# A second chunk of attention in plain float32 products, with the softmax sums taken by the value product

## The chip, the cores and the metric

The kernel runs on one core of a Trainium2 chip. The metric is the device time of one execution in microseconds (us); lower is better. The core has a matrix engine (PE, with its weight loads listed apart as PEld), three engines for elementwise work (DVE, ACT and POOL), and SP, which here issues nearly all of the DMA transfers.

## The reference

Causal window attention with sink keys, and behind it an expert network on every token, all in float32:

```
q, k, v: [4 batches, 8 heads, 768 positions, 64]
keep = (key < n_sink) or (0 <= query - key < window)      # n_sink 4, window 128
scores = where(keep, q @ k.T / 8, -1e9)
scores = scores - max(scores)
a = exp(scores);  a = a / (sum(a) + 1e-9)
x = (a @ v) with the heads side by side                   # 3072 tokens x 512
h = x @ w_in                                              # 512 x 2048
r = maximum(h, 0)
out = (s * r * r + b) @ w_out                             # 2048 x 512; s, b scalars
```

## The kernel before, in words

The 3072 tokens are cut into 8 chunks of 384 (`CH`): chunk c is half c % 2 of batch c // 2, that is three blocks of 128 queries for each of 8 heads. A chunk has an attention part and a network part. The program runs the attention of chunk 0 alone, and then for each chunk its network with the attention of the next chunk woven in: `moe_steps` gives the network as a list of steps, the attention gives a list of slots, and the loop at the end of the kernel puts slots behind steps in proportion. A *stage* below is one chunk's network with what is woven into it. The last stage hides nothing.

The network of a chunk walks over 16 blocks `f` of 128 hidden units. A step `l1` makes `h` (L521) from two operands, a high and a low part of x (`x_0` and `x_1`), by three products; ACT takes the Relu (L524), DVE and ACT make g and its low part (L525, L527, L528), and `l2` adds three products of g with the second weight into three PSUM tiles `po` (L539), which leave at the end of the chunk through `ot` (L543). The products are in the type fp32r, to which an operand is rounded; the low part holds what the rounding of the high part left off.

The weights come packed in 16 tiles of 1 MB, one for each `f`, and are loaded once (`load_weight`, L171, on SP's queue). They too must be split, half a tile at a time. ACT converts and scales (L198, L199), DVE combines (L200, L201), POOL adds (L203), ACT casts the high part (L208), and DVE or POOL subtracts for the low part (L214). A few of the tiles are decoded in the first part of the program, and the rest in stage 0, a step or two ahead of their use. In the listings w_261, w_263, w_265, w_267, w_269, w_452, w_454 and w_456 are tiles 0 to 7. Tiles 8 and up get other names, in order: w_647, w_714, w_800 before, and w_604, w_678, w_736, w_793, w_851, w_933 after.

There are two forms of attention. `attn_slots`, for chunks 1 to 7, splits q, k and v into fp32r parts (L268 to L278, with L272 on DVE and L273 and L278 on POOL), scores only the keys of the window and the sinks (272 columns, L293 and L294), masks and takes the row minimum in one DVE instruction (L298), exponentiates with the sum in the same ACT instruction (L304), transposes (L316, L317), splits the transposed probabilities (L321 on ACT, L322 on DVE), multiplies with V (L354), and divides and splits the result (L362, L363, L382, L383). A chunk that is a second half has more value products (six blocks of keys rather than five).

`first_slots`, for chunk 0, uses plain float32 products on the unsplit operands. For each head and block of queries (a *unit*, 24 in all) `fa` makes the scores of all keys up to that block, 128, 256 or 384 (L443), masks them with a dense mask `m_full` and leaves the row minimum in `negm` (L445, followed by a small instruction that reads the accumulator), and exponentiates (L449, the sum into `zz`). At the end of a head `fn` adds 1e-9, takes the reciprocal of its three sums, and multiplies the three probability tiles by it (L457, L458, L460). `fb` transposes a unit and copies it (L468, L472), `fc` multiplies with V (L480, three products) and splits the result into x's two parts (L482, L483). `fb` and `fc` run `LB0` and `LC0` slots behind `fa`.

The order in which instructions stand on each engine comes from a scheduler that works from the program's order, its dependences and a table of costs. On an engine the instructions run in that order. SBUF is cut into pools: `wk` for work tiles, whose tags give a ring of buffers each; `first` for what only chunk 0's attention needs; and `late`, which is opened when `first` is closed and lies in the same place. The weight tiles from 8 on are in `late`, so their loads can't start before chunk 0's attention is done with `first`.

```
for i, f in enumerate(slots):            # slots of chunk 0
    f()
    if i == 10: weights(4, 0)            # loads of the first weight tiles
    if i == 18: constants2()
    if i >= 22 and i % 2 == 0:
        weights(NEARLY - 1, (i - 20) // 2)
first_cm.__exit__(None, None, None)      # then late is opened
```

Of the kernel before, what the change touches and what calls it, by code (L numbers as in the profile page):

```python
# [38 lines left out]
def tile_kernel(ctx, tc, qT, kT, k0, v, vsk, n_sink, window, w, s, b, out):  # L39
# [376 lines left out]
    def first_slots():  # L416
        k = Chunk()

        q = [wk.tile([P, NCC, CH], F32, tag=f"x{i}", name=f"q0{i}") for i in range(2)]
# [4 lines left out]

        def load():
            nc.gpsimd.memset(q[0][D:], 0.0)
            nc.vector.memset(q[1][:D], 0.0)
# [8 lines left out]

        def fa(h, i):
            pr = h // 2
# [1 line left out]
            u = h * BLK + i  # L440
# [1 line left out]
            sc = psO.tile([P, 512], F32, tag="po", name="sc0")
            nc.tensor.matmul(sc[:, :n], q[h % 2][:, pr, i * P:(i + 1) * P], kk[:, pr, :n], start=True, stop=True)  # L443
            sm = first.tile([P, CH], F32, name="sm0", tag="sm0", bufs=E0)
            nc.vector.tensor_tensor_reduce(out=sm[:, :n], in0=sc[:, :n], in1=m_full[i], scale=-0.125, scalar=BIG,  # L445
                                           op0=ALU.add, op1=ALU.min, accum_out=negm[:, uu])
# [2 lines left out]
            nc.scalar.activation(sm[:, :n], sm[:, :n], AF.Exp, bias=negm[:, uu], scale=-1.0, accum_out=zz[h][:, 0, i:i + 1])  # L449
            sms[(h, i)] = sm  # L450

        def fn(h, i):

            n = (i + 1) * P
            z = zz[h]
            if i == 0:
                nc.vector.tensor_scalar(out=z[:, 1], in0=z[:, 0], scalar1=1e-9, scalar2=None, op0=ALU.add)  # L457
                nc.vector.reciprocal(out=z[:, 0], in_=z[:, 1])  # L458
# [1 line left out]
            nc.vector.tensor_scalar(out=sm[:, :n], in0=sm[:, :n], scalar1=z[:, 0, i:i + 1], scalar2=None, op0=ALU.mult)  # L460

        def fb(h, i):
            sm = sms.pop((h, i))
            if i == 0:
# [7 lines left out]
            nc.scalar.copy(out, tp[:, :(i + 1) * P].rearrange("p (k c) -> p k c", c=P))  # L472

        def fc(h):
            pr, hs = h // 2, slice(h % 2 * D, (h % 2 + 1) * D)
            o = ps("o0")
            t = tt.pop(h).rearrange("p k c -> p (k c)")
            for kb in range(BLK):
                c0 = kb * 3 * P
                nc.tensor.matmul(o[:, kb * P:CH], vv[:, pr, kb * P:(kb + 1) * P], t[:, c0:c0 + (BLK - kb) * P],  # L480
                                 start=(kb == 0), stop=(kb == BLK - 1))
# [263 lines left out]
```

## Time and profile before

| | us |
|---|---|
| median of 3 runs | 781.66 |
| lowest, highest | 780.46, 782.41 |
| the profiled execution's own time | 781.77 |
| its span, from first to last instruction | 780.0 |
| PE busy | 735.3 (94%) |
| PEld busy | 656.9 (84%) |
| DVE busy | 513.6 (66%) |
| ACT busy | 495.5 (64%) |
| POOL busy | 268.8 (34%) |

The profile is of one execution. A group line of it names the source line, the engine, the operation, the output and input tiles with their shape (partitions x elements) and count; behind the bar stand the busy time, the mean duration of one in ns, and the idle time of the engine just before these instructions with what ended most of it. A window line gives a stretch of the span, its length, and the busy us of PE, PEld, DVE, ACT and POOL with the count of instructions, then the granted clock of PE as a share of full speed, the DMA engines' busy share and GB/s. A timeline line gives start, duration, engine, line and operation, and in brackets how long the engine had been idle and what released it. A line on one group's durations gives least, median and largest in ns, and when the first and the last of them ran.

### The profile page before, as it was taken

How to read it: one execution, taken by the hardware profiler on the slowest of the kernel's cores; microseconds unless marked ns; L12 is line 12 of the kernel's file. 1: busy time of each engine (PE TensorE's matmuls, PEld its weight loads, DVE VectorE, ACT ScalarE, POOL GpSimd, SP SyncE). 2: the span in 40 equal slices, each digit the busy share in tenths (PEclk: the TensorE clock that was granted, in tenths of full speed). 3: DMA queues.
4: the chain of work that ended last, by engine and by line, in shares of the span. 5: the costliest groups of instructions: out<-in, count | busy, mean ns of one | idle time of the engine just before them, and what ended most of it. 6: DMA issues, size and time to landing. Idle time of an engine off the chain costs nothing.

```text
span 780.0 us, 12112 instructions
## 1 busy us (share of the span) xinstructions
PE 735.3 (94%) x4036; PEld 656.9 (84%) x4036; DVE 513.6 (66%) x1250; ACT 495.5 (64%) x1231; POOL 268.8 (34%) x411
## 2 busy tenths in 40 slices
PE   7977988699999999999999999999999999999996
PEld 4655776579999999899999999899989999899985
DVE  6879998985676467655676466665676466663231
ACT  4886977766666576656666576656666576643222
POOL 3057668652343233322243233332343233210000
PEclk9989999999999999999999999999999999999998
DMA  7636205212112212112112212112111212001001
GB/s 271 273 103 229 105 14 170 76 34 77 42 54 59 73 43 67 35 43 76 43 53 57 76 43 62 40 43 76 43 53 55 77 43 60 21 1 42 1 1 45
DMA packets 28118, 54.21 MB, mean 70 GB/s; under 512 B 3600, under 2 KB 16528, under 8 KB 26128
## 3 DMA queue, kind: packets, MB, share of 16 engines
q1 hardware_dynamic: 28048, 53.36, 21.3%
q8 instruction: 34, 0.56, 0.3%
q14 instruction: 36, 0.29, 0.1%
HBM read 47.06 MB, written 6.29 MB: 68 GB/s over the span
## 4 chain that ended last, share of the span: by engine, by line
PE 76%; DVE 8%; ACT 7%; issue 3%; POOL 3%; DMA 2%; SPq 1%; ACTq 0%; POOLq 0%; DVEq 0%
PE h L521 30%; PE po L539 30%; PE o L354 5%; PE sc L294 2%; PE sc L293 2%; PE tp L317 2%; PE tp L316 2%; ACT w L199 1%; DVE r L525 1%; DMA w<-in_w 1%; PE o L480 1%; POOL w L203 1%; DVE w L201 1%; DVE qs L272 1%; ACT sm L304 1%
## 5 line engine op out<-in xcount | busy, mean ns | idle before, releaser
L521 PE MATMUL h<-x,w 128*128 128x384 f32 x1536 | 299.5, 343 | 8.7 <-DVE hl L322 3.8
L539 PE MATMUL po<-w,g 128*128 128x512 f32 x1152 | 301.6, 403 | 5.7 <-ACT g L527 3.7
L521 PEld LDWEIGHTS h<-x,w 128*128 128x128 f32 x1536 | 269.7, 190 | 14.5 <-issue 4.0
L539 PEld LDWEIGHTS po<-w,g 128*128 128x128 f32 x1152 | 211.6, 191 | 47.7 <-ACT g L527 4.9
L524 ACT ACTIVATE r<-h 128x384 f32<-128x384 f32 x128 | 62.9, 491 | 103.9 <-PE h L521 96.9
L298 DVE CUSTOM_DVE_ANT_0 sm<-sc,msk 128x272 f32<-128x272 f32 (+1 forms) x168 | 70.2, 418 | 78.4 <-PE sc L294 55.9
L525 DVE SCALAR_TENSOR_TENSOR r<-r,sb 128x384 f32<-128x384 f32 x128 | 84.1, 657 | 54.1 <-ACT r L524 54.0
L528 DVE SCALAR_TENSOR_TENSOR g<-r,sb,g 128x384 fp32r<-128x384 f32 x128 | 85.5, 668 | 45.6 <-ACT g L527 43.5
L305 POOL COPY psk<-sm 128x48 f32<-128x48 f32 x168 | 52.2, 311 | 162.9 <-ACT sm L304 161.7
L304 ACT ACTIVATE sm<-sm,negm 128x272 f32<-128x272 f32 (+1 forms) x168 | 85.4, 508 | 23.3 <-DVE negm L298 22.3
L527 ACT ACTIVATE g<-r,sb 128x384 fp32r<-128x384 f32 x128 | 78.7, 614 | 33.2 <-DVE r L525 32.1
L273 POOL TENSOR_TENSOR kl<-kraw,kh 128x544 fp32r<-128x544 f32 (+1 forms) x56 | 74.9, 1337 | 56.8 <-ACT kh L271 55.5
L321 ACT CAST hl<-tp 128x256 fp32r<-128x256 f32 (+1 forms) x168 | 58.8, 352 | 26.4 <-PE tp L317 26.2
L354 PE MATMUL o<-hl,vv 128*128 128x256 f32 (+1 forms) x400 | 71.4, 295 | 1.1 <-DVE hl L322 0.8
L322 DVE TENSOR_TENSOR hl<-tp,hl 128x256 fp32r<-128x256 f32 (+1 forms) x168 | 66.8, 398 | 7.5 <-ACT hl L321 6.7
L278 POOL TENSOR_TENSOR vv<-vraw,vv 128x256 fp32r<-128x256 f32 (+1 forms) x56 | 41.9, 747 | 60.9 <-ACT vv L277 59.0
L354 PEld LDWEIGHTS o<-hl,vv 128*128 128x128 f32 x400 | 54.9, 190 | 2.7 <-DVE hl L322 1.1
L293 PE MATMUL sc<-kh,qs 128*128 128x272 f32 (+1 forms) x168 | 47.8, 284 | 5.8 <-DVE hl L322 4.7
L363 DVE TENSOR_TENSOR xm<-o,y 64x384 f32<-64x384 f32 x56 | 31.0, 553 | 31.5 <-ACT y L362 31.3
L294 PE MATMUL sc<-kl,qs 128*128 128x272 f32 (+1 forms) x168 | 48.5, 289 | 0.0
L203 POOL TENSOR_TENSOR w<-w 128x1024 int32<-128x1024 int32 (+1 forms) x17 | 32.6, 1921 | 42.4 <-DVE z L458 19.3
L317 PE MATMUL tp<-identr,sm 128*128 128x128 f32 x168 | 45.7, 272 | 0.0
(112 smaller groups left out, 852.0 us busy)
## 6 DMA issues: line engine op xcount, KB each, us to landing
w<-in_w SPq DMA_DIRECT2D x15, 1024.0 KB, 8.9
kraw<-in_kT SPq DMA_DIRECT2D x32, 272.0 KB, 2.7
out<-ot SPq DMA_DIRECT2D x24, 256.0 KB, 2.0
qraw<-in_qT SPq DMA_DIRECT2D x28, 192.0 KB, 2.4
kraw<-in_kT SPq DMA_DIRECT2D x24, 208.0 KB, 2.4
vraw<-in_v SPq DMA_DIRECT2D x16, 256.0 KB, 2.7
vraw<-in_v SPq DMA_DIRECT2D x12, 192.0 KB, 2.3
vsraw<-in_vsk SPq DMA_DIRECT2D x28, 64.0 KB, 1.8
```

The costliest lines, as they stand in the source:

```text
L273: nc.gpsimd.tensor_tensor(out=hd.kl[:, :kw], in0=hd.k[:, :kw], in1=hd.kh[:, :kw].bitcast(F32), op=ALU.subtract)
L293: nc.tensor.matmul(sc[:, :n], hd.qs[:, qs], hd.kh[:, c0:c0 + n], start=True, stop=False)
L294: nc.tensor.matmul(sc[:, :n], hd.qs[:, qs], hd.kl[:, c0:c0 + n], start=False, stop=True)
L298: nc.vector.tensor_tensor_reduce(out=sm[:, :n], in0=sc[:, :n], in1=m, scale=-0.125, scalar=BIG, op0=ALU.add, op1=ALU.min, accum_out=negm[: ...
L304: nc.scalar.activation(sm[:, :n], sm[:, :n], AF.Exp, bias=negm[:, uu], scale=-1.0, accum_out=pp.zz[:, i, hh:hh + 1])
L322: nc.vector.tensor_tensor(out=lo, in0=tp[:, a:z], in1=hi.bitcast(F32), op=ALU.subtract)
L354: nc.tensor.matmul(hd.o[:, q0:q0 + n * P], hd.vv[:, kb, :], hd.hl[:, t, c0 * P:(c0 + n) * P], start=(hd.n == 0), stop=(i == BLK - 1 and kb ...
L521: nc.tensor.matmul(h[:, :CH], weight[f][:, 0, wi, cc * P:(cc + 1) * P], x[xi][:, cc, :], start=(i == 0), stop=(i == 11))
L525: nc.vector.scalar_tensor_tensor(out=r, in0=r, scalar=s_ap, in1=r, op0=ALU.mult, op1=ALU.mult)
L527: nc.scalar.activation(gg[:, 0, :], r, AF.Identity, bias=b_ap, scale=1.0)
L528: nc.vector.scalar_tensor_tensor(out=gg[:, 1, :], in0=r, scalar=b_ap, in1=gg[:, 0, :].bitcast(F32), op0=ALU.add, op1=ALU.subtract)
L539: nc.tensor.matmul(po[tb], gg[:, gi, tsl], weight[f][:, 1, wi, :], start=(f == 0 and i == 0), stop=(f == NF - 1 and i == 2))
```

## The change

The second chunk to be computed becomes chunk 2, the first half of batch 1, and its attention is done with plain float32 products as chunk 0's is. The chunks now run in the order 0, 2, 1, 3, 4, 5, 6, 7, so stage 0 hides the attention of chunk 2, stage 1 (chunk 2's network) that of chunk 1, and stage 2 (chunk 1's network) that of chunk 3.

`first_slots` becomes `plain_slots(c)`, used for chunks 0 and 2. In it the normalisation moves. Before, the 24 probability tiles of a chunk were multiplied by 1/sum ahead of the transpose. Now V's tile for a head has 128 columns, 64 of values and 64 of ones (the ones in columns 64 to 127 for even heads and in 0 to 63 for odd ones), so the value product leaves the head's output in 64 partitions of PSUM and the sum, 64 times over, in the other 64. `fc` adds 1e-9 to the sums, takes their reciprocal (64 x 384 elements) and multiplies the output by it, once per head. The high and the low part of x are then made once per pair of heads, by a cast on ACT and a subtraction on POOL. The exponential takes no sum any more. `fb` and `fc` for chunk 0 run 3 and 5 slots behind `fa`, where it was 4 and 6.

V is loaded for chunk 0 in 8 pieces, one for each head, with 64 values (256 bytes) to a row, where there were 2 pieces. For chunk 2 `load_pair` issues two loads of q, one of k and two of v per pair of heads, and POOL fills the zeros beside q and the ones beside v. Chunk 2's tiles take the rings that the split attention's tiles have (`kh`, `qs`, `vv`, `sm`, `kl`, `hl`, `xm`, `y`). The dense mask `m_all` moves out of the pool `first` into `wk` (tag `xsk`).

```diff
-E0, LB0, LC0 = 8, 4, 6
+E0, LB0, LC0 = 8, 3, 5
+ORDER = 0, 2, 1, 3, 4, 5, 6, 7
...
-    m_all = first.tile([P, 6 * P], MDT, tag="m", name="m_all")
+    m_all = wk.tile([P, 6 * P], MDT, tag="xsk", name="m_all", bufs=1)
...
-    def first_slots():
+    def plain_slots(c):
+        k.c, bb = c, c // 2
...
+        if c == 0:
+            q0 = [wk.tile([P, NCC, CH], F32, tag=f"x{i}", name=f"q0{i}") for i in range(2)]
+            k0_ = first.tile([P, NCC, CH], F32, tag="k0", name="k0")
+            v0 = first.tile([P, NCC, BLK, 2, P], F32, tag="v0", name="v0")
...
+        def halves(h):
+            own, other = slice(0, D), slice(D, P)
+            return (own, other) if h % 2 == 0 else (other, own)
...
-                nc.sync.dma_start(vv[:, ps_, :].rearrange("p r (n e) -> p r n e", n=BLK),
-                                  v[0, ps_, :, :BLK].rearrange("r p n h d -> p r n (h d)"))
+                for pr in range(rs.start, rs.stop):
+                    for hh in range(2):
+                        hs = slice(hh * D, (hh + 1) * D)
+                        nc.sync.dma_start(v0[:, pr, :, hh, hs], v[0, pr, :, :BLK, hh, :])
+        def ones():
+            for hh in range(2):
+                nc.gpsimd.memset(v0[:, :, :, hh, (1 - hh) * D:(2 - hh) * D], 1.0)
+        def load_pair(pr):
+            kt = wk.tile([P, 544], F32, tag="kh", name="k_p")
+            nc.sync.dma_start(kt[:, :CH], k0[bb, :, pr, :])
+            for hh in range(2):
...
+                q[h] = wk.tile([P, CH], F32, tag="qs", name="q_p")
+                nc.gpsimd.memset(q[h][other], 0.0)
+                nc.sync.dma_start(q[h][own], qT[bb, pr, own, :CH])
+                vv[h] = wk.tile([P, 4, P], F32, tag="vv", name="v_p", bufs=VB)
+                nc.gpsimd.memset(vv[h][:, :BLK, other], 1.0)
+                nc.sync.dma_start(vv[h][:, :BLK, own], v[bb, pr, :, :BLK, hh, :])
         def fa(h, i):
...
-            nc.scalar.activation(sm[:, :n], sm[:, :n], AF.Exp, bias=negm[:, uu], scale=-1.0, accum_out=zz[h][:, 0, i:i + 1])
+            k.last = nc.scalar.activation(sm[:, :n], sm[:, :n], AF.Exp, bias=negm[:, uu], scale=-1.0)
-        def fn(h, i):
-            n = (i + 1) * P
-            z = zz[h]
-            if i == 0:
-                nc.vector.tensor_scalar(out=z[:, 1], in0=z[:, 0], scalar1=1e-9, scalar2=None, op0=ALU.add)
-                nc.vector.reciprocal(out=z[:, 0], in_=z[:, 1])
-            sm = sms[(h, i)]
-            nc.vector.tensor_scalar(out=sm[:, :n], in0=sm[:, :n], scalar1=z[:, 0, i:i + 1], scalar2=None, op0=ALU.mult)
         def fc(h):
...
-                nc.tensor.matmul(o[:, kb * P:CH], vv[:, pr, kb * P:(kb + 1) * P], t[:, c0:c0 + (BLK - kb) * P],
+                nc.tensor.matmul(o[:, kb * P:CH], vv[h][:, kb, :], t[:, c0:c0 + (BLK - kb) * P],
                                  start=(kb == 0), stop=(kb == BLK - 1))
-            nc.scalar.copy(k.x[0][hs, pr, :], o[hs, :CH])
-            nc.vector.tensor_tensor(out=k.x[1][hs, pr, :], in0=o[hs, :CH], in1=k.x[0][hs, pr, :].bitcast(F32), op=ALU.subtract)
+            if h % 2 == 0:
+                xs[pr] = wk.tile([P, CH], F32, tag="xm", name="xm_p")
+            y = wk.tile([P, CH], F32, tag="y", name="y_p", bufs=1)
+            nc.vector.tensor_scalar(out=y[own], in0=o[other, :CH], scalar1=1e-9, scalar2=None, op0=ALU.add)
+            nc.vector.reciprocal(out=y[own], in_=y[own])
+            nc.vector.tensor_tensor(out=xs[pr][own], in0=o[own, :CH], in1=y[own], op=ALU.mult)
+            if h % 2 == 1:
+                x = xs.pop(pr)
+                nc.scalar.copy(k.x[0][:, pr, :], x)
+                nc.gpsimd.tensor_tensor(out=k.x[1][:, pr, :], in0=x, in1=k.x[0][:, pr, :].bitcast(F32), op=ALU.subtract)
...
+        lb, lc = (LB0, LC0) if c == 0 else (2, 4)
+        ahead = {max(2 * BLK * pr - 3, 0): pr for pr in range(H // 2)} if c else {}
...
-    k, slots = first_slots()
+    k, slots = plain_slots(0)
...
-    for c in range(NC_):
+    for j, c in enumerate(ORDER):
...
-            k, slots = attn_slots(c + 1)
+            k, slots = (plain_slots if j == 0 else attn_slots)(ORDER[j + 1])
```

The host's array `k0`, keys by pair of heads, is given for two batches instead of one. Lines of the kernel after lie a little further down: L445 becomes L481 (the masked score), L449 L484 (the exponential), L472 L499 (the transposed copy), L524 and L527 L561 and L564, and those of `load_weight` and `make_weight` by one.

The scheduler puts the instructions in another order. On DVE, in the middle of chunk 0's attention, three heads in, this stood (`sc` scores, `sm` probability tiles, `z` sums of one head; an ISA row with `negm` alone reads the accumulator):

```order
L445 ISA negm 128x1
L457 TENSOR_SCALAR z_172<-z_172 128x3
L445 ISA sm_210,negm<-sc_208,m_all 128x256
L445 ISA negm 128x1
L458 RECIPROCAL z_172<-z_172 128x3
L460 TENSOR_SCALAR sm_170<-sm_170,z_172 128x128
L460 TENSOR_SCALAR sm_176<-sm_176,z_172 128x256
L460 TENSOR_SCALAR sm_185<-sm_185,z_172 128x384
L445 ISA sm_219,negm<-sc_217,m_all 128x384
```

and this stands there after (`o` is the value product of a head, `y_p` its sums, `xm_p` the output of a pair):

```order
L513 TENSOR_SCALAR y_p<-o_216 64x384
L481 ISA sm_237,negm<-sc_235,m_all 128x128
L481 ISA negm 128x1
L514 RECIPROCAL y_p<-y_p 64x384
L481 ISA sm_246,negm<-sc_244,m_all 128x256
L481 ISA negm 128x1
L515 TENSOR_TENSOR xm_p<-o_216,y_p 64x384
L481 ISA sm_273,negm<-sc_271,m_all 128x384
```

The normalisation has moved from ahead of the transpose to behind the value product, between the masked scores of a later head.

On ACT, around the first step of the network (the first `r<-h` row is the Relu of block 0, `g` its result), this stood:

```order
L198 ACTIVATE w_263<-w_263 128x1024
L482 CAST x_0_104<-o_517 64x384
L199 ACTIVATE w_263<-w_263 128x1024
L268 CAST qs<-qraw 64x384
L277 CAST vv<-vraw 128x4x64
L198 ACTIVATE w_456<-w_456 128x1024
L524 ACTIVATE r<-h 128x384
L304 ACTIVATE sm,zz<-sm,negm 128x272
L208 CAST w_586<-w_261 128x2x512
L524 ACTIVATE r<-h 128x384
L527 ACTIVATE g<-r,sb 128x384
```

and this stands there after (`x_0_106` is the high part of chunk 0's x, its last pair):

```order
L199 ACTIVATE w_736<-w_736 128x1024
L200 ACTIVATE w_736<-w_736 128x1024
L199 ACTIVATE w_793<-w_793 128x1024
L209 CAST w_595<-w_269 128x2x512
L518 CAST x_0_106<-xm_p 128x384
L484 ACTIVATE sm_p<-sm_p,negm 128x256
L200 ACTIVATE w_793<-w_793 128x1024
L199 ACTIVATE w_851<-w_851 128x1024
L561 ACTIVATE r<-h 128x384 x2
L209 CAST w_669<-w_452 128x2x512
L564 ACTIVATE g<-r,sb 128x384 x2
```

Before, the passes over tiles 1 and 7 stood ahead of the first Relu; now those over tiles 8 to 12 do (the rows ahead of these have w_604 and w_678).

On SP, around the loads of the weights from tile 8 on, this stood:

```order
L171 DMA w_647<-in_w 128x2048
L250 DMA kraw<-in_kT 128x544
L235 DMA qraw<-in_qT 128x384
L237 DMA vraw<-in_v 128x512
L171 DMA w_714<-in_w 128x2048
L250 DMA kraw<-in_kT 128x544
L171 DMA w_800<-in_w 128x2048
```

and after:

```order
L251 DMA kraw<-in_kT 128x544
L172 DMA w_604<-in_w 128x2048
L172 DMA w_678<-in_w 128x2048
L172 DMA w_736<-in_w 128x2048
L172 DMA w_793<-in_w 128x2048
L172 DMA w_851<-in_w 128x2048
L172 DMA w_933<-in_w 128x2048
L464 DMA q_p<-in_qT 64x384 x2
L457 DMA k_p<-in_k 128x384
```

The loads of tiles 8 to 13 now stand in one row; before, loads of the next chunk's keys stood between them, and loads of q and v.

More of the change, by code (lines that the diff above doesn't have):

```diff
@@ new lines, in load_all @@
+                for pr in range(rs.start, rs.stop):
[9 more added lines that the diff above has]
+            for hh in range(2):
+                h = 2 * pr + hh
+                own, other = halves(h)
+                kk[h] = kt
+                q[h] = wk.tile([P, CH], F32, tag="qs", name="q_p")
[4 more added lines that the diff above has]
+                nc.sync.dma_start(vv[h][:, :BLK, own], v[bb, pr, :, :BLK, hh, :])
@@ L437, in fa @@
         def fa(h, i):
[L438 removed]
             n = (i + 1) * P
[L440 removed]
+            u = (c * H + h) * BLK + i
             uu = slice(u, u + 1)
[L442 to L444 removed]
+            sc = psO.tile([P, 512], F32, tag="po", name="sc0") if c == 0 else ps("sc0")
@@ L470, in fb @@
             t0, c0 = i // 2, i % 2 * P
-            out = tt[h][:, t0:t0 + i + 1, c0:c0 + P]
-            nc.scalar.copy(out, tp[:, :(i + 1) * P].rearrange("p (k c) -> p k c", c=P))
+            nc.scalar.copy(tt[h][:, t0:t0 + i + 1, c0:c0 + P], tp[:, :(i + 1) * P].rearrange("p (k c) -> p k c", c=P))
         def fc(h):
-            pr, hs = h // 2, slice(h % 2 * D, (h % 2 + 1) * D)
+            pr = h // 2
+            own, other = halves(h)
             o = ps("o0")
@@ L494, in f @@
                     nc.sync.dma_start(sb[:, 1:2], b.partition_broadcast(P))
+                if t in ahead:
+                    load_pair(ahead[t])
                 if t < n:
                     fa(*units[t])
-                if t % BLK == BLK - 1 and t < n:
-                    for i in range(BLK):
-                        fn(t // BLK, i)
-                if 0 <= t - LB0 < n:
-                    fb(*units[t - LB0])
-                if 0 <= t - LC0 < n and (t - LC0) % BLK == BLK - 1:
-                    fc((t - LC0) // BLK)
+                if 0 <= t - lb < n:
+                    fb(*units[t - lb])
@@ L505, in slot @@
+                if 0 <= t - lc < n and (t - lc) % BLK == BLK - 1:
+                    fc((t - lc) // BLK)
             return f
-        return k, [slot(t) for t in range(n + LC0)]
+        return k, [slot(t) for t in range(n + lc)]
     def moe_steps(x, store, wk, before=None, last=False):
```

59 lines of the change are left out of this document (35 added, 24 removed).

## The prediction

> **What bounds the kernel now.** First the windows of the three parts of the program, then when each chunk's last output leaves, then the operations of the part that is not full. A stage here is one chunk's expert network (steps of `l1` and `l2`) with the next chunk's attention between the steps; stage 0 holds chunk 0's network. The columns are window, its length, then busy microseconds of PE, PEld, DVE, ACT and POOL, the granted clock, DMA share and GB/s.
>
> ```profile
> 7.00:49.50 42.50, 32.80 (x146) 22.79 (x144) 31.54 (x117) 33.79 (x92) 8.54 (x13) 0.90 0.60 232
> 49.50:177.50 128.00, 104.00 (x519) 86.61 (x519) 119.34 (x196) 99.78 (x201) 85.82 (x76) 0.94 0.33 112
> 177.50:264.00 86.50, 86.03 (x494) 79.27 (x493) 55.60 (x148) 55.91 (x152) 28.04 (x53) 1.00 0.19 55
> 264.00:353.30 89.30, 88.97 (x518) 82.19 (x517) 57.57 (x148) 58.23 (x152) 29.60 (x53) 1.00 0.18 55
> ```
>
> From 177.5 on PE is busy to within half a microsecond of each window: those stages last as long as their matmuls. Stage 0 is different: DVE 119.3 of 128 (93%), PE 104 at a clock of 0.94. There DVE is the bound, because the weights are decoded there beside the attention. In the first part (chunk 0's attention alone) no engine is over 80%: it is a chain through DVE, ACT and PE.
>
> The stage ends, from the timeline (start, length, engine, line): the last output copy of chunks 0, 1 and 2.
>
> ```profile
> 179.01 0.60 ACT L543 ACTIVATE ot<-po 128x512 f32<-128x512 f32 x1 [1.26 <-DMA out<-ot]
> 265.44 0.60 ACT L543 ACTIVATE ot<-po 128x512 f32<-128x512 f32 x1 [1.25 <-DMA out<-ot]
> 354.83 0.60 ACT L543 ACTIVATE ot<-po 128x512 f32<-128x512 f32 x1 [1.25 <-DMA out<-ot]
> 717.80 2.12 PE h L521 x12
> 719.91 2.11 PE po L539 x9
> ```
>
> The stage that hides a first half's attention (chunk 2) lasts 86.4, the one that hides a second half's (chunk 3) 89.4: 3.0 more. The last two lines (chain of waits, last chunk) give the network itself: 16 x (2.12 + 2.11) = 67.7.
>
> **Part 1: stage 0 loses the split attention.** Groups of DVE within 49.5 to 176, listed busy and mean; L445 and L460 are those of chunk 0's attention, over the whole span:
>
> ```profile
> L201 DVE SCALAR_TENSOR_TENSOR w<-w,wt 128x1024 int32<-128x1024 int32 (+1 forms) x15 | 17.3, 1157 | 0.1
> L528 DVE SCALAR_TENSOR_TENSOR g<-r,sb,g 128x384 fp32r<-128x384 f32 x16 | 16.0, 997 | 1.1 <-ACT g L527 1.1
> L272 DVE TENSOR_TENSOR qs<-qraw,qs 64x384 fp32r<-64x384 f32 x9 | 12.1, 1343 | 0.3
> L298 DVE CUSTOM_DVE_ANT_0 sm<-sc,msk 128x272 f32<-128x272 f32 x24 | 10.4, 432 | 0.5 <-PE sc L294 0.3
> L322 DVE TENSOR_TENSOR hl<-tp,hl 128x256 fp32r<-128x256 f32 x24 | 9.9, 414 | 0.1
> L363 DVE TENSOR_TENSOR xm<-o,y 64x384 f32<-64x384 f32 x8 | 4.4, 550 | 0.1
> L445 DVE CUSTOM_DVE_ANT_0 sm<-sc,m_all 128x128 f32<-128x128 f32 (+2 forms) x24 | 9.3, 417 | 1.6 <-PE sc L443 1.5
> L214 DVE TENSOR_TENSOR w<-w,w 128x1024 fp32r<-128x1024 f32 (+1 forms) x12 | 14.7, 1226 | 0.8 <-ACT w L208 0.7
> L460 DVE TENSOR_SCALAR sm<-sm,z 128x128 f32<-128x128 f32 (+2 forms) x24 | 9.4, 447 | 0.1
> L483 DVE TENSOR_TENSOR x<-o,x 64x384 fp32r<-64x384 f32 x1 | 0.6, 565 | 0.0
> ```
>
> ```profile
> 49.50:176.00 126.50, 102.50 (x512) 85.42 (x512) 118.78 (x195) 98.53 (x198) 85.65 (x75) 0.94 0.33 112
> L445 DVE DVE_READ_ACCUMULATOR2_ANT negm<- 128x1 f32 x24 | 2.0, 81 | 0.0
> L528 DVE SCALAR_TENSOR_TENSOR g<-r,sb,g x128: 599/619/2133, 59.9 to 768.2; 128x384 fp32r<-128x384 f32 x128
> ```
>
> The window's 20 DVE groups, from L201 (17.3) to L483 (0.6), list 129.6; the split attention's are 49.2 of it (L272, L298, L322 and L363, and 12.4 in eight smaller groups). Added is the plain attention: the masked score 9.3 plus 2.0 of accumulator reads (the L445 group is the same 24 units, from chunk 0), and per head a 64x384 add and a 64x384 multiply at 0.55 (as L363) and a 64x384 reciprocal R: 11.3 + 8 x 1.1 + 8R = 20.1 + 8R. By the order two of the weights' low parts (L214, 1.23 each) now stand behind chunk 0's last score: 2.5.
>
> R is shown nowhere at this size. Nearest are the reciprocals of 3 and 6 elements a partition:
>
> ```profile
> L458 DVE RECIPROCAL z<-z x8: 160/175/178, 10.2 to 41.5; 128x3 f32<-128x3 f32 x8
> L328 DVE RECIPROCAL zr<-zr x28: 173/190/192, 80.3 to 691.2; 128x6 f32<-128x6 f32 x28
> ```
>
> Medians 175 and 190 ns: 5 ns an element; minima 4.3. At 4.6 R = 0.175 + 381 x 4.6 ns = 1.9 us, my value. Lower end: as any other pass, 0.56. Upper end: largest of six against smallest of three, 10.7 ns an element, 4.2 us. The Trainium skill (VectorE: DVE Perf Modes, section on the fixed hardware budget) says that reciprocal runs an iterative divide with a repeat count of 8; read as 8 cycles an element at its 0.96 GHz that would be an estimated 3.35 us, and the sum below would come to about 783. The step from three to six elements here is 15 ns, where 8 cycles would be 25, so the trace agrees only by half.
>
> Listed DVE work of stage 0 then is 129.6 - 49.2 + 20.1 + 2.5 + 8R = 103.0 + 8R = 118.2. Listings overlap (129.6 listed are 118.8 busy in that window's row, 0.917): 108.4. POOL loses the key, value and copy passes beside which DVE's own ran longer: L528 took 997 ns here in the mean against 619 in the median of all 128; I give back 5. So 103.4.
>
> PE goes up. Float32 products take two passes, each at half the pace:
>
> ```profile
> 27.15 1.46 PE L480 MATMUL o<-tt,v 128*128 128x384 f32 x6
> 28.45 0.49 PE L468 MATMUL tp<-identr,sm 128*128 128x128 f32 x3
> 28.78 1.47 PE L443 MATMUL sc<-k,q 128*128 128x128 f32 x6
> ```
>
> A head's six value passes hold PE 1.30 (27.15 to 28.45), its scores, six passes too and as many columns (1.47 listed, as against 1.46), the same, and three transposes 0.33 (28.45 to 28.78), six 0.66: 3.3 a head, 26.5 for eight. The split second half costs 89.4 - 67.7 = 21.7. So stage 0 needs 67.7 + 26.5 = 94.2 of PE at full clock, 5 more than it did. ACT, at 99.8, falls: its split parts go, only exponentials, copies and one cast a pair come. POOL's new 64-partition fills wait for PE to release the q and v buffers, with the weight additions (L203) queued behind; they are released one to two steps before those additions' results are used, so I cost them at nothing; if that slack is gone, each costs a step's wait of 2 to 3 us.
>
> **Part 2: chunk 0's attention, and the hole behind it.** Normalising leaves the chain between exponential and transpose (L460, 9.4, and two small operations a head), and the sum's accumulator reads leave ACT. But the order fills ACT: up to the last score copy now stand 14 unsigned-to-float and scale passes of weights (6 before) beside the same exponentials and copies.
>
> ```profile
> 8.07 0.40 ACT L449 ACTIVATE sm<-sm,negm 128x128 f32<-128x128 f32 x1 [3.21 <-DVE negm L445]
> L449 ACT ACTIVATE sm<-sm,negm 128x128 f32<-128x128 f32 (+2 forms) x24 | 12.2, 508 | 3.7 <-DVE negm L445 3.6
> L472 ACT COPY tt<-tp 128x128 f32<-128x128 f32 (+2 forms) x24 | 8.5, 370 | 2.9 <-PE tp L468 2.6
> L199 ACT ACTIVATE w<-w 128x1024 f32<-128x1024 f32 x13 | 15.0, 1156 | 0.0
> L208 ACT CAST w<-w 128x1024 fp32r<-128x1024 f32 x13 | 14.7, 1130 | 9.4 <-POOL w L203 8.1 <-DVE w L214 1.2
> L383 ACT CAST x<-xm 128x384 fp32r<-128x384 f32 x28 | 14.3, 510 | 8.4 <-DVE xm L382 8.4
> L524 ACT ACTIVATE r<-h 128x384 f32<-128x384 f32 x128 | 62.9, 491 | 103.9 <-PE h L521 96.9
> L527 ACT ACTIVATE g<-r,sb 128x384 fp32r<-128x384 f32 x128 | 78.7, 614 | 33.2 <-DVE r L525 32.1
> 16.70 1.10 ACT L198 ACTIVATE w<-w 128x1024 int32<-128x1024 uint32 x1 [2.94 <-DMA w<-in_w]
> 57.84 0.96 PE L539 MATMUL po<-w,g 128*128 128x512 f32 x3 [1.09 <-ACT g L527]
> DMA to landing us min/median/max: 8.9/14.1/18.2
> DMA to landing us min/median/max: 4.9/4.9/4.9
> 20.00:22.00 2.00, 2.00 (x7) 1.30 (x7) 1.10 (x6) 2.00 (x6) 0.00 (x0) 0.55 1.03 434
> ```
>
> 12.2 + 8.5 + 14 x 1.16 + two casts 1.0 + 1.13 = 39.0 listed, some 33.5 held (0.86, an estimate: ACT's short passes overlap somewhat more than DVE's 0.917). From the first exponential at 8.1, with the 7.6 of gaps that ACT has now in that part (42.5 - 33.8 less 1.1 ahead of its start; the 2.94 wait for the first weight among them) and the last product, T0, the end of chunk 0's attention, is about 51, against 49.5. V's pieces of 256 B could add up to 3 (its 0.79 MB at half of the 248 GB/s that the window 4 to 6 had).
>
> Behind T0 comes the hole. Weight tiles 8 to 13 (w_604 to w_933 in the order) lie where the first pool was, so their loads go at T0. The row with 4.9 is such a load alone; the seven of the start, issued 7.8 to 13.4, landed 16.7 to 31.6, 2.48 apart. ACT now has the passes of tiles 8 to 12 ahead of the first Relu: nine passes, three high-part casts, two exponentials, the last pair's cast, two Relus and one Identity, 16.8 listed, 15 held, after a 5.1 wait: the first `po` product is at T0 + 20 = 71, where it now is at 57.84. In that time PE has three `h` groups and three scores (7.7); after such a gap the clock row reads 0.55, which I cost at 1. The Trainium skill (TensorE: Matmul & The Clock Gate, What's actually happening) says that an idle window of about 3.4 us halves the clock and a busy one restores it: the trace agrees, and that sentence makes the same 1 to 2 us.
>
> With DVE idle for about 4 in the hole, behind the Relu, two bounds follow. From 71 on PE has 13 x 2.12 + 16 x 2.11 + 26.5 - 1.3 = 86.5 left; at the 93% that DVE reaches now, 93: end at 164. DVE by itself: 51 + 4 idle + 103.4/0.93 = 166. With both near full and the clock's 1, **stage 0 ends at 168** where it ended at 177.5: -9.5.
>
> **Part 3: the other stages.** Stage 1 hides a second half's attention instead of a first half's: +3.0. Everything later is the same multiset of stages. Before the handover the last pair's add, reciprocal, multiply, cast and low part take R and four passes of 0.5 to 1 us, 4 to 5 in all, covered by the last `po` group and a first `h` group (4.2); a dear reciprocal would show there as a microsecond or two.
>
> **Sum.** 781.77 - 9.5 + 3.0 = 775.3 for the profiled execution (span 780.0 and 1.8 around it, median 781.66): **775**. A measurement of this kernel tells about 0.3%, 2.3 us.
>
> **Rivals.** Dear reciprocal, slower: at the upper end of 4.2 the DVE work is 103.0 + 33.6 listed, 120.3 held after the same steps; with T0 2 later and no idle left, 53 + 120.3/0.93 = 182, which is +4.5 + 3.0 and 789. It decides from R = 3.3 on, where stage 0 ends at 174.5. For it speaks that no row shows a long reciprocal; against it the 15 ns. 0.22.
>
> The gain is spent in the hole, no change: if T0 is 55 (V's small pieces, ACT's waits) and weights land late, the first `po` is at 78, 94 more make 172 to 173, and the time 780. For it: ACT is in order, and 2.94 of it already went to one landing. 0.18.
>
> PE alone binds: R near 0.56, T0 at 48: 68 + 86.5/0.95 = 159, or 162 with the clock and a wait: 766 to 770. Against it: the slope of the two rows. 0.15. The forecast has 0.45.
>
> **How the numbers follow.** The forecast's own range is 771 to 779. Faster by over 0.3%: the forecast nearly whole (0.42), PE alone 0.15, a little of the hole 0.03: 0.60. Same: 0.11 of the hole, 0.05 of the dear reciprocal, 0.03 of the forecast: 0.19. Slower: 0.21. The range leaves out the ends of the first and last rival: 767 to 788.
>
> **What would show it.** A reciprocal of 64x384 near 1.9; the first `po` at about 71, behind an ACT that reads tiles 8 to 12 first; the end of stage 0 near 168 with DVE and PE both over 85% after 71; chunk 2's stage at 89.4; later stages unchanged. Wrong if the reciprocal is over 3, if T0 is beyond 54, or if POOL's fills hold the weight additions.

## The result and the profile after

The kernel after takes 791.56 us in the median of 4 executions (790.69 to 792.27), the kernel before 781.26 in the same comparison: ratio 1.013, interval 1.0112 to 1.0148. It is 10.3 slower, where 775 was forecast. The profiled execution took 790.69, with a span of 788.9.

First the ends of the stages, from ACT's timeline of the kernel after: the last output copies of chunks 0, 2 and 1.

```profile
185.35 0.60 ACT L580 ACTIVATE ot<-po 128x512 f32<-128x512 f32 x1 [0.35 <-DMA out<-ot]
274.32 0.60 ACT L580 ACTIVATE ot<-po 128x512 f32<-128x512 f32 x1 [1.22 <-DMA out<-ot]
363.79 0.60 ACT L580 ACTIVATE ot<-po 128x512 f32<-128x512 f32 x1 [1.23 <-DMA out<-ot]
```

Against 179.01, 265.44 and 354.83 before, chunk 0 ends 6.3 later, the next stage takes 89.0 instead of 86.4, and the third 89.5 instead of 89.4. So all of the loss, some 9 us between these two executions, is there before 274, and 6.3 of it before 185. Three windows of the kernel after (columns as in the prediction) and three rows of groups show the part before 185: the first part, the stretch from the last value product of chunk 0 to the first output product `po`, and the rest of stage 0.

```profile
7.00:50.30 43.30, 29.97 (x140) 21.17 (x140) 36.46 (x87) 34.42 (x67) 8.74 (x16) 0.94 0.73 242
50.30:78.70 28.40, 15.62 (x49) 11.81 (x47) 28.09 (x26) 16.41 (x21) 15.78 (x8) 0.67 0.56 226
78.70:183.90 105.20, 94.52 (x441) 77.71 (x442) 95.29 (x136) 59.04 (x115) 45.93 (x35) 0.95 0.17 55
L513 DVE TENSOR_SCALAR y_p<-o x16: 550/553/560, 14.9 to 180.7; 64x384 f32<-64x384 f32 x16
L514 DVE RECIPROCAL y_p<-y_p x16: 2530/2548/2550, 15.7 to 181.3; 64x384 f32<-64x384 f32 x16
L515 DVE TENSOR_TENSOR xm_p<-o,y_p x16: 544/555/561, 18.5 to 183.9; 64x384 f32<-64x384 f32 x16
```

The reciprocal takes 2.55 us. In the middle window DVE is busy for 28.09 of 28.40 us, while PE has 15.6 of work at a granted clock of 0.67: the hole that the prediction expected is there, but DVE fills it. DVE's timeline shows with what, and PE's three rows what waits for it. (L201, L202 and L215 are passes over the weights, L215 the low part; L513, L514 and L515 are the add, the reciprocal and the multiply of the new normalisation; L561, L562 and L564 are the Relu, the square and g of the network; L518 and L519 make the high and the low part of x on ACT and POOL. Rows left out are marked by dots.)

```profile
49.33 2.55 DVE L514 RECIPROCAL y_p<-y_p 64x384 f32<-64x384 f32 x1
...
56.32 2.53 DVE L514 RECIPROCAL y_p<-y_p 64x384 f32<-64x384 f32 x1
...
62.12 2.55 DVE L514 RECIPROCAL y_p<-y_p 64x384 f32<-64x384 f32 x1
64.70 1.23 DVE L215 TENSOR_TENSOR w<-w,w 128x1024 fp32r<-128x1024 f32 x1
65.95 0.56 DVE L515 TENSOR_TENSOR xm_p<-o,y_p 64x384 f32<-64x384 f32 x1
...
66.89 3.53 DVE L201 TENSOR_SCALAR wt<-w 128x1024 int32<-128x1024 int32 x2
70.34 3.15 DVE L202 SCALAR_TENSOR_TENSOR w<-w,wt 128x1024 int32<-128x1024 int32 x2
73.41 2.38 DVE L201 TENSOR_SCALAR wt<-w 128x1024 int32<-128x1024 int32 x1
75.71 2.77 DVE L562 SCALAR_TENSOR_TENSOR r<-r,sb 128x384 f32<-128x384 f32 x2
65.98 2.65 PE L558 MATMUL h<-x,w 128*128 128x384 f32 x7 [5.59 <-DVE w L215]
71.33 3.25 PE L558 MATMUL h<-x,w 128*128 128x384 f32 x9 [2.70 <-POOL x L519]
78.66 1.84 PE L576 MATMUL po<-w,g 128*128 128x512 f32 x5 [2.10 <-ACT g L564]
```

Chunk 0's last value product ends at 50.3, but the reciprocals of its last three heads start at 49.33, 56.32 and 62.12, with weight passes between them. PE waits 5.59 us for one of these passes, the low part of a weight tile that stands behind the last reciprocal. The last head's output is ready at 66.5. ACT casts it; POOL first finishes a weight pass of its own and makes the low part of x from 69.82 to 71.27; then PE can go on with `h` at 71.33. The squares (L562) stand behind five more weight passes. The first `po` comes at 78.66, where it came at 57.84. So the reciprocals are not the whole of the hole: DVE's and POOL's weight passes lie in the same chain.

### The profile page after: what moved, and what is told of

It reads as the page before. It is cut to its first block, busy times and chain, and to the rows that moved or that the text cites. A ratio compares the mean times of both kernels' runs of the same rounds, so it can differ in the third digit from the quotient of the medians.

```text
span 788.9 us, 11898 instructions
## 1 busy us (share of the span) xinstructions
PE 741.1 (94%) x4024; PEld 660.4 (84%) x4024; DVE 525.3 (67%) x1182; ACT 474.4 (60%) x1139; POOL 249.9 (32%) x385
## 4 chain that ended last, share of the span: by engine, by line
PE 76%; DVE 11%; ACT 6%; issue 3%; POOL 2%; DMA 1%; SPq 0%; ACTq 0%; POOLq 0%; DVEq 0%
PE h L558 30%; PE po L576 30%; PE o L355 5%; PE sc L295 2%; PE sc L294 2%; DVE y_p L514 2%; PE tp L318 2%; PE tp L317 2%; DVE r L562 2%; DVE wt L201 1%; DVE w L202 1%; POOL w L204 1%; ACT w L199 1%; ACT w L200 1%; DVE w L215 1%
## 5 line engine op out<-in xcount | busy, mean ns | idle before, releaser
L558 PE MATMUL h<-x,w 128*128 128x384 f32 x1536 | 302.2, 346 | 11.2 <-DVE w L215 6.1
L561 ACT ACTIVATE r<-h 128x384 f32<-128x384 f32 x128 | 62.7, 490 | 115.7 <-PE h L558 108.7
L562 DVE SCALAR_TENSOR_TENSOR r<-r,sb 128x384 f32<-128x384 f32 x128 | 86.7, 678 | 60.0 <-ACT r L561 60.0
L299 DVE CUSTOM_DVE_ANT_0 sm<-sc,msk 128x272 f32<-128x272 f32 (+1 forms) x144 | 61.0, 423 | 77.7 <-PE sc L295 62.7
L565 DVE SCALAR_TENSOR_TENSOR g<-r,sb,g 128x384 fp32r<-128x384 f32 x128 | 82.3, 644 | 44.0 <-ACT g L564 41.9
L564 ACT ACTIVATE g<-r,sb 128x384 fp32r<-128x384 f32 x128 | 78.5, 615 | 32.1 <-DVE r L562 31.3
L306 POOL COPY psk<-sm 128x48 f32<-128x48 f32 x144 | 38.2, 266 | 162.6 <-ACT sm L305 161.5
L305 ACT ACTIVATE sm<-sm,negm 128x272 f32<-128x272 f32 (+1 forms) x144 | 73.6, 511 | 19.9 <-DVE negm L299 19.1
L274 POOL TENSOR_TENSOR kl<-kraw,kh 128x544 fp32r<-128x544 f32 (+1 forms) x48 | 61.9, 1290 | 54.1 <-ACT kh L272 52.5
L322 ACT CAST hl<-tp 128x256 fp32r<-128x256 f32 (+1 forms) x144 | 51.2, 356 | 28.6 <-PE tp L318 28.1
L323 DVE TENSOR_TENSOR hl<-tp,hl 128x256 fp32r<-128x256 f32 (+1 forms) x144 | 58.0, 402 | 7.9 <-ACT hl L322 7.1
L355 PE MATMUL o<-hl,vv 128*128 128x256 f32 (+1 forms) x352 | 61.8, 294 | 0.0
L279 POOL TENSOR_TENSOR vv<-vraw,vv 128x256 fp32r<-128x256 f32 (+1 forms) x48 | 34.5, 718 | 54.5 <-ACT vv L278 52.1
L514 DVE RECIPROCAL y_p<-y_p 64x384 f32<-64x384 f32 x16 | 40.7, 2544 | 0.3
L294 PE MATMUL sc<-kh,qs 128*128 128x272 f32 (+1 forms) x144 | 40.6, 282 | 0.0
```

The source lines that it names most:

```text
L274: nc.gpsimd.tensor_tensor(out=hd.kl[:, :kw], in0=hd.k[:, :kw], in1=hd.kh[:, :kw].bitcast(F32), op=ALU.subtract)
L323: nc.vector.tensor_tensor(out=lo, in0=tp[:, a:z], in1=hi.bitcast(F32), op=ALU.subtract)
L355: nc.tensor.matmul(hd.o[:, q0:q0 + n * P], hd.vv[:, kb, :], hd.hl[:, t, c0 * P:(c0 + n) * P], start=(hd.n == 0), stop=(i == BLK - 1 and kb ...
L558: nc.tensor.matmul(h[:, :CH], weight[f][:, 0, wi, cc * P:(cc + 1) * P], x[xi][:, cc, :], start=(i == 0), stop=(i == 11))
L561: nc.scalar.activation(r, h[:, :CH], AF.Relu, scale=1.0 / WUP)
L562: nc.vector.scalar_tensor_tensor(out=r, in0=r, scalar=s_ap, in1=r, op0=ALU.mult, op1=ALU.mult)
```

## The experiments

Three things could have cost the time: the reciprocals (theory A, as first put: DVE's sum of work bounds all of stage 0), or the loads and weight passes in the hole (B), or chunk 2's products on PE (C). The table has the medians of all runs but `prices` against about 781.5 for the kernel before; the kernels are described below it. The scheduler puts each kernel in order anew, so every run changes the order along with what its edit says; and by the intervals a difference of two medians is uncertain by some 2 to 3 us.

| kernel | median us | ratio to before (interval) | first `po` | chunk 0's last copy |
|---|---|---|---|---|
| after | 791.56 | 1.013 (1.0112 to 1.0148) | 78.66 | 185.35 |
| norec | 771.60 | 0.9879 (0.9862 to 0.9895) | 57.00 | 165.90 |
| pairrec | 777.16 | 0.9948 (0.9932 to 0.9964) | 62.31 | 173.52 |
| oldnorm | 776.30 | 0.993 (0.9913 to 0.9946) | 52.93 | 175.33 |
| c0only | 796.58 | 1.0199 (1.0182 to 1.0217) | 77.05 | 191.11 |
| ordered | 792.00 | 1.0122 (1.009 to 1.0153) | 72.70 | 188.22 |
| c2only | 775.72 | 0.9916 (0.9889 to 0.9943) | 57.84 | 171.59 |
| mix | 778.51 | 0.9963 (0.9949 to 0.9977) | 56.25 | 174.07 |
| notail | 782.67 | 1.0018 (0.9998 to 1.0039) | 66.47 | 178.06 |
| nohead | 782.47 | 1.0008 (0.9995 to 1.0022) | 67.55 | 178.53 |
| noc2 | 788.48 | 1.0077 (1.0053 to 1.0101) | 80.61 | 184.80 |
| orderonly | 784.27 | 1.0032 (1.0017 to 1.0047) | 56.60 | 178.97 |
| no0 | 771.89 | 0.9862 (0.9833 to 0.989) | 60.87 | 167.19 |
| c2norec | 777.31 | 0.9939 (0.9916 to 0.9961) | 57.49 | 175.34 |

**norec: the reciprocals left out.**

```diff
-            nc.vector.reciprocal(out=y[own], in_=y[own])
```

> The kernel after without the 16 reciprocals: y stays the sum plus 1e-9, and the head's output is multiplied by it. Theory A (DVE bounds stage 0, and the eleven reciprocals that run inside it, 28.0 us of DVE, are what made it longer): stage 0 has 26 us less of DVE held, so PE binds; first output product near 68 instead of 78.7, last output copy of chunk 0 near 161 instead of 185.35, whole execution 767 (762 to 772). Theory B (the hole is made by the loads of weight tiles 8 to 13, which wait for the end of chunk 0's attention, and by ACT's passes over them): first output product stays at 75 or later, chunk 0 ends at 170 or later, 777 to 783. Theory C (PE's float32 products bind from 78.7 on, where PE is busy 90%): the hole shrinks but the 104 us behind it stay, chunk 0 ends near 173, 779 to 783.

It took 771.60, 20.0 less than the kernel after and at the upper end of A's range. The first `po` came at 57.0, 11 earlier than A said, but chunk 0 ended at 165.90, 5 later: the hole shrank more than A had it, and the rest of the stage not at all (108.9 from the first `po` to the last copy, 106.7 in the kernel after). That was the first sign against A. So the reciprocals cost the time, and the loads of tiles 8 to 13, which still wait for chunk 0's end, do not make a hole of that size on their own. B and C fall as first causes.

**pairrec: one reciprocal a pair.** The sums of both heads of a pair go to the two halves of one tile; ACT copies each head out of PSUM.

```diff
...
-            nc.vector.reciprocal(out=y[own], in_=y[own])
-            nc.vector.tensor_tensor(out=xs[pr][own], in0=o[own, :CH], in1=y[own], op=ALU.mult)
+            nc.scalar.copy(xs[pr][own], o[own, :CH])
             if h % 2 == 1:
+                nc.vector.reciprocal(out=y, in_=y)
+                nc.vector.tensor_tensor(out=xs[pr], in0=xs[pr], in1=y, op=ALU.mult)
```

> One reciprocal of 128x384 for each pair of heads instead of two of 64x384; ACT copies the unnormalised head out of PSUM, and one 128x384 multiply for a pair. Theory A: if the reciprocal costs by elements in a partition, it is 2.55 again and there are 8 of them; about 5 or 6 fewer in stage 0, 13 to 15 us less of DVE held there with the multiply, chunk 0 ends near 170, 776 (771 to 781). Theory B: first output product at 75 or later, no gain over 4 us: 786 to 791. Theory C: 783 to 791.

777.16, as A said, and faster than the kernel before.

```profile
L517 DVE RECIPROCAL y_p<-y_p x8: 2539/2550/2554, 23.8 to 169.2; 128x384 f32<-128x384 f32 x8
```

The row of its reciprocals shows the same 2.55 us for 128 partitions as for 64.

**oldnorm: the old normalisation in both plain chunks.** The functions are those of the kernel before (`fn`, sums from the exponential, x's parts made per head); order and plain products are those of the kernel after. `fb` and `fc` run 4 and 6 slots behind `fa` in chunk 0, as before, and 3 and 5 in chunk 2 (2 and 4 in the kernel after).

> Chunk 2 second and in plain float32 products as in the kernel after, but both plain chunks normalised as in the kernel before: exponential with its sum, 24 multiplies by 1/sum ahead of the transpose, the two parts of x made for each head from PSUM. Theory A: DVE has 12.7 us a chunk less than with the reciprocals, and chunk 0's tail of three heads does not fall into stage 0: 20 us less of DVE held there, chunk 0 ends at 162 to 168, 769 to 775, faster than both kernels. Theory B: the same loads wait at the same place, first output product at 75 or later, 780 or more. Theory C: PE has the same products, 779 to 785.

776.30: better than both kernels, but 1 to 7 behind what A said, and chunk 0 ends at 175.33, not 162 to 168. This was another sign against A. PE's list of waits in its stage 0 has this at the top:

```profile
PE tp L507 <- DVE sm_p L495: 11.7, 7, 2.9
```

Chunk 2's transposes wait 11.7 us for the old multiplies, with DVE busy for 103.9 of 129 us: this looks like waits in order rather than DVE's sum, but no run takes these waits alone away.

**c0only: chunk 0's new form alone.** Natural order of chunks, all others in split products (`ORDER = 0, 1, 2, ...`, and `attn_slots` for chunk 1).

> Chunks in their natural order, all but chunk 0 in split products; chunk 0 alone with the ones beside V and the reciprocals. Theory A: three of chunk 0's reciprocals with their adds and multiplies, 11 us of DVE, fall into stage 0, which DVE bounds already: chunk 0 ends 8 to 11 later than in the kernel before, 788 to 793. Theories B and C (loads, or chunk 2's products): stage 0's own work is that of before, so 780 to 784.

796.58: 15.0 more than before and 4 beyond A's range, without any of chunk 2's part. First `po` at 77.05.

**ordered: the weight passes moved out of the hole.**

```diff
...
     def before(f):
-        weights(f + 2 + LOADS // 2, 2 * f + 5)
+        if f == 0: weights(f + 2 + LOADS // 2, 2 * f + 5)
+        else:      # issued behind the first Relu (ACT) and the first square (DVE)
+            with tc.issue_after(mark[0]), tc.issue_after(mark[1]):
+                weights(f + 2 + LOADS // 2, 2 * f + 5)
```

> The kernel after with one thing moved: the weight passes that the second and later network steps call for stand behind the first Relu on ACT and behind the first square on DVE, so that tiles 8 to 12 are no longer read ahead of the first step. Every operation is kept. Theory A (DVE's sum of work bounds stage 0): the first output product comes some 10 us earlier, near 68, but chunk 0 still ends at 182 to 187, and the execution takes 787 to 793. Rival B (the passes that the scheduler put into the hole cost the time): chunk 0's end moves with the first output product, 173 to 176, 778 to 783.

792.00, no change, as A said, though the first `po` came 6 earlier (72.70; A had 68). Its windows ahead of that product and behind it:

```profile
49.00:72.70 23.70, 15.09 (x42) 10.31 (x43) 19.37 (x20) 7.56 (x12) 8.24 (x4) 0.64 0.55 222
72.70:187.00 114.30, 97.48 (x460) 78.20 (x459) 108.94 (x143) 76.89 (x134) 54.71 (x40) 0.97 0.19 61
```

The passes taken out of the hole come back behind it: DVE has 108.9 there, against 95.3 in the kernel after, and that stretch is 9.0 longer. PE has 2.9 us more work there, and its `h` products wait 8.3 us for low parts of weights (5.4 from DVE, 2.9 from POOL), against 0.2 in the kernel after. So the passes are not free behind the first `po` either, and their order in the hole was not what cost the time.

**c2only: chunk 0 as before, chunk 2 as after**, and **orderonly: the kernel before in the new order.**

> Chunk 0 exactly as in the kernel before (sums by the exponential, 24 multiplies), chunk 2 second and as in the kernel after, with its 8 reciprocals of 64x384. Theory A: stage 0 has eight reciprocals, not eleven, and no tail of chunk 0; from the kernel after, 12 us of DVE less, chunk 0 ends at 172 to 175, 778 to 781. Rival (chunk 2's float32 products and its loads are what cost): no better than the kernel after, 787 or more.

> The kernel before with the chunks in the order 0, 2, 1, 3 and on, and nothing else: chunk 2 in split products. Stage 1 hides a second half and takes 89 instead of 86.4; stage 0 hides a first half (fewer keys and values to split, fewer value products) and gets up to 2 shorter, since its DVE work hardly changes: 782 to 785. Rival (a half's value products count in stage 0 as in stage 1): stage 0 shorter by 3, 781.

c2only took 775.72, 15.8 less than the kernel after, and has the lowest median of the kernels that leave nothing out (oldnorm's is within the noise). A had 778 to 781: it took too little for chunk 0's part. orderonly took 784.27: the order by itself costs 2.9. Its chunks 0 and 2 end at

```profile
178.97 0.60 ACT L544 ACTIVATE ot<-po 128x512 f32<-128x512 f32 x1 [1.26 <-DMA out<-ot]
268.38 0.60 ACT L544 ACTIVATE ot<-po 128x512 f32<-128x512 f32 x1 [1.26 <-DMA out<-ot]
```

so stage 0 stays as it was and stage 1 takes 89.4 instead of 86.4. The three parts of the change are then: order +2.9, chunk 2 in plain products -8.5 (784.27 to 775.72), chunk 0's new form +15.8 (to 791.56). The last holds all that changed in chunk 0, not the reciprocals alone: also V's eight loads, the shorter distances of `fb` and `fc`, and what the new form saves.

**mix: chunk 0 as before, one reciprocal a pair in chunk 2.**

> Chunk 0 as in the kernel before, chunk 2 in plain float32 products with one reciprocal of 128x384 for a pair of heads. Theory A: four reciprocals in stage 0 and no tail of chunk 0, so less DVE there than in either form alone; chunk 0 ends at 168 to 172, 772 to 776. Rival (PE and the chain through chunk 2's units bind once DVE is under 90%): no better than one reciprocal a pair in both chunks, 776 to 779.

778.51, a miss for A and in its rival's range: four reciprocals fewer than c2only, and 2.8 slower. Why it is slower and not equal was not isolated; it also has eight more copies on ACT.

**prices: the reciprocal by itself.** Durations from the timeline of a kernel before with the list of operations in it:

> The kernel before with a list of operations behind its last chunk, each twice: reciprocals of 64 partitions by 24, 96, 192 and 384 elements and of 128 by 384, multiplies of 64x384 and 128x384, and a logarithm and an exponential of 128x384 on ACT. From 175 ns for 3 elements, 190 for 6 and 2548 for 384: 0.153 us and 6.24 ns for each element in a partition, so 0.30, 0.75, 1.35, 2.55 and again 2.55 for 128 partitions. Rival: 5 ns an element as the two short rows alone say, with a larger fixed part for long ones: then 192 elements would take more than 1.45.

```profile
L688 DVE RECIPROCAL pb<-pa x8: 294/1038/2536, 702.0 to 720.3; 64x24 f32<-64x24 f32 x2, 64x96 f32<-64x96 f32 x2, 64x192 f32<-64x192 f32 x2, 64x384 f32<-64x384 f32 x2
703.58 1.33 DVE L688 RECIPROCAL pb<-pa 64x192 f32<-64x192 f32 x1
L689 DVE RECIPROCAL pb<-pa x2: 2535/2544/2553, 707.8 to 723.2; 128x384 f32<-128x384 f32 x2
```

294 ns for 24 elements, 1.33 us for 192, 2.54 for 384: 6.2 ns for each element in a partition and 0.15 us fixed, the same for 64 and 128 partitions. The Trainium skill (VectorE: DVE Perf Modes, section on the fixed hardware budget) has a repeat count of 8 for it; read as 8 cycles at the page's 0.96 GHz that is an estimated 8.3 ns an element, or 3.35 us with the fixed part. The measured 6.2 ns stands against that reading.

**notail, nohead, noc2: parts of the reciprocals left out.** Chunk 0's last three (in the hole), chunk 0's first five, chunk 2's eight; the output of those heads is multiplied by the sum.

```diff
-            nc.vector.reciprocal(out=y[own], in_=y[own])
+            if c or h < 5:      # notail;  c or h >= 5: nohead;  not c: noc2
+                nc.vector.reciprocal(out=y[own], in_=y[own])
```

> The kernel after without the reciprocals of chunk 0's last three heads, which run behind its last value product (the output of those heads is multiplied by the sum). Theory A (what runs once DVE has become the bound is paid in full): 7.6 us of reciprocals, some 8 of stage 0, chunk 0 ends at 176 to 178, 782 to 785. Rival (each of the 16 reciprocals costs the same sixteenth of the 20 us that leaving all out gained): 3.7 less, 787 to 789.

> The kernel after without the reciprocals of chunk 0's first five heads, 12.7 us of DVE. Theory A: they lie in the first part, where DVE is at 84% and the chain through DVE, ACT and PE sets the pace; the end of chunk 0's products comes up to 6 earlier (43.7 instead of 50.3 where all reciprocals are left out) and the rest follows as it was: 785 to 788. Rival (all alike): 6.3 less, 785. If DVE's sum is all that counts from the start of the program: 13 less, 778.

> The kernel after without the eight reciprocals of chunk 2, 20.4 us of DVE in stage 0. Theory A: paid in full until PE and the chains bind, which they do at 166 where all are left out; with chunk 0's tail still there chunk 0 ends at 168 to 171, 774 to 778. Rival (all alike): 10 less, 781 to 782.

notail gained 8.9 for 7.6 us of reciprocals, nohead 9.1 for 12.7 (A had 4 to 7), noc2 only 3.1 for 20.4 (788.48, where A had 774 to 778). That ends theory A. The windows behind the first `po`, of noc2 and of the kernel after:

```profile
80.60:183.00 102.40, 92.52 (x440) 78.08 (x440) 81.00 (x128) 58.99 (x116) 47.47 (x36) 0.95 0.17 55
78.70:184.00 105.30, 94.62 (x441) 77.81 (x442) 95.39 (x136) 59.04 (x115) 45.93 (x35) 0.95 0.18 55
```

14.4 us less of DVE (20.4 of reciprocals went, but other passes ran longer, such as L202's eleven, 13.3 for 11.2), and the stretch is 2.9 shorter; PE has nearly the same work in both. So theory D was put in A's place: ahead of the network's first output product DVE sets the pace, and its work there is paid in full; behind it PE, at a granted clock of 0.95 and with waits in order (an engine stands at an instruction whose input is not ready), sets the pace, and DVE's work is covered. PE's list of waits in that stretch of the kernel after agrees with the second half: 12.4 us in all, of which 1.8 end with an instruction of DVE and the rest with ACT. Two runs set limits to it: in nohead 9.1 of 12.7 us were paid, which is less than full, and in ordered the weight passes, for which `h` waits, were not covered.

**no0 and c2norec: a test of theory D.** All eight reciprocals of chunk 0 left out; and c2only without chunk 2's eight.

> The kernel after without chunk 0's eight reciprocals, chunk 2's eight kept. Theory D (up to the network's first output product DVE sets the pace, and its work there is paid in full; behind it PE and its chains do, and DVE's work is covered): chunk 0's reciprocals cost what the two parts did, 9.1 + 8.9 us, so 773 to 775, with the first output product at 57 to 60. Theory A (DVE's sum up to the end of stage 0): 20.4 us of DVE in chunk 0 are worth as much as the same 20.4 us in chunk 2, which brought 3.1: 785 or more.

> Chunk 0 as in the kernel before, chunk 2 second in plain float32 products, its eight reciprocals left out (the heads are multiplied by the sum). Theory D: they run behind the first output product, where 20.4 us of DVE brought 3.1 in the kernel after; here, with DVE at 109 of 112 us behind that product, up to 5: 770 to 773. Theory A (DVE's sum, 109 of 112 us there): 20.4 less DVE is worth 10 or more until PE binds: 766 or less.

no0 took 771.89: chunk 0's eight reciprocals alone cost 19.7 of their 20.4 us. That is 1.7 more than the 18.0 of their two parts, no more than noise, and puts the time 1.1 below D's range; first `po` and chunk 0's end both moved by 18 (60.87, where D had 57 to 60, and 167.19). A's 785 is out. c2norec took 777.31: leaving chunk 2's eight out of c2only gained nothing (it is 1.6 slower, within the noise, where D had 3 to 6 faster): they are covered more fully than D said, and A's 766 is out. So both runs decide between A and D, though neither time lies in D's range. Windows of no0, c2only and c2norec from about 58 on (no0's begins 2.9 ahead of its first `po`, the others at theirs) to 1 to 3 ahead of chunk 0's last copy:

```profile
58.00:166.00 108.00, 95.65 (x455) 78.29 (x455) 104.42 (x142) 71.87 (x128) 53.14 (x38) 0.97 0.28 93
57.80:170.00 112.20, 97.54 (x458) 80.89 (x457) 109.25 (x145) 72.83 (x130) 54.39 (x40) 0.95 0.25 86
58.00:172.00 114.00, 97.91 (x446) 81.31 (x447) 95.06 (x137) 72.40 (x130) 52.68 (x40) 0.93 0.24 81
```

DVE's sum there goes from 95 to 109 without the length following it; the longest has the least DVE. PE has 96 to 98 in all three. So DVE's sum does not set the length there. That PE with its waits does is argued from these rows: no run takes work from PE alone, and why no0's window is 6 shorter than c2norec's was not isolated.

## Why the prediction was wrong, point by point

- **The step that failed: Part 2, T0 and the hole.** That part summed chunk 0's attention on ACT alone and said that normalising leaves the chain. Nowhere does the sum charge chunk 0's own eight reciprocals: R stands in Part 1 only, 8 times, for chunk 2. By its own numbers (1.1 + R a head, at R = 1.9) 24 us of DVE were added to chunk 0, against 9.4 of multiplies and 4.5 of low parts taken out. T0 came out nearly right (50.3 for 51), but by luck: without chunk 0's reciprocals, which the sum left out, the last value product ends at 43.7 (norec) or 46.0 (no0). And T0 times the products alone; at that moment three heads' normalisation was still to be done, and the first product that needs it could not start. "DVE idle for about 4 in the hole" was 0.3 of 28.4. The runs put 19.7 us on chunk 0's reciprocals (no0) and 15.8 on its whole new form (c2only against the kernel after).
- **The reciprocal's price** was 2.55 for 1.9. The value was chosen from a slope of 4.6 ns; the two rows' minima and medians were too coarse for the 6.2 that it is. By the prediction's own sum 0.65 more, 8 times, is 5.2 listed and at most 5 of time; the runs show that for chunk 2's eight even the whole price is nearly covered (3.1 in noc2, nothing in c2norec). The size was off, but the place mattered more: at 2.55 the prediction's sum would have come to 781 at most.
- **The hole.** First `po` forecast 71, seen 78.66. ACT does read tiles 8 to 12 first, as was said, but neither this nor the loads set the hole (norec: 57.0 with the same loads; ordered: no gain in time with the passes moved). DVE's chain through the last three heads did, with the weight passes that stand between them (notail: first `po` 12.2 earlier for 7.6 us of reciprocals).
- **Stage 0 bound by DVE.** Forecast as DVE 103.4, at 93%. It held 123.4 in 133.6 us (92%). The difference is the tail of chunk 0 (three times 3.65, 11 listed) and the reciprocal's size (5.2 listed); 118.2 and these are 134.4 listed, 123.2 at 0.917, so of the 5 given back for POOL's lighter work nothing came: the mean of g's low part (L528, now L565) fell from 997 to 802 ns, but that of the square (L525, now L562) rose from 903 to 1116, 16 of each. But the view was too simple: 92% over the stage is full in the hole (99%) and not binding behind it (91%, and 14 us less shorten it by 2.9).
- **Chunk 2 in plain products, and the order.** Together they were forecast at -6.5. c2only, which is just these two, has -5.9 (775.72 against 781.65). Stage 1 was forecast +3.0 and has +2.5 here, +3.0 in orderonly. This half of the forecast was right in time, but in good part by luck: in c2only the first `po` comes at 57.84, not 71, and the rest of stage 0 takes 114, not 97, two errors that nearly cancel. And its reason, DVE's sum, is not what sets that rest (c2norec).
- **The rivals.** The dear reciprocal was said to decide from 3.3 on; the time passed even its 789 at 2.55, since that rival too charged chunk 2's eight alone, and 2 us of T0. The gain spent in the hole had the place right (first `po` at 78), for another reason (V's small pieces; T0 was not late), and gave 780. PE alone binding fits the stretch behind the first `po` better than DVE's sum does, though PE waits there too; but it asked for a first `po` at 68, 11 earlier than it came.

## What to carry to other kernels

Count a new instruction at every place where the changed function is called, and ask for each place separately what sets the pace there: the same 2.55 us eight times cost 19.7 in a stretch that nothing else covered, and 0 to 3 behind the first `po`, where PE was busy for 90% and its waits seldom ended with DVE. A busy share over a stage (92%) can be the mean of a stretch at 99% that is paid and one at 91% that is not. If a sum has to be inverted, do it where it is short (3 elements a partition, 0.17 us) and not after it has been spread over 384, at least where nothing covers it: in chunk 2, behind the first `po`, the two forms differ by 0.6 us (c2only and oldnorm), which is within the noise.

## What the runs showed of the hardware

The reciprocal costs 6.2 ns for each element in a partition, 64 or 128 partitions alike (2.55 us for 384), while a multiply or an add of the same shape takes 0.55. A logarithm and an exponential that follow each other on ACT each came behind a table load of 1.28 us in prices, which would outweigh the 0.52 of the operation itself.
